# Half of the row maxima from scores and relu of key differences, the gate on GpSimd and ScalarE early, output weights stored one at a time

## The chip, the cores and the metric

The kernel runs on one core of one Trainium2 chip. The metric is the device time of one execution in microseconds (us); the median of three runs is given. Five engines work side by side, each through its own instructions in order: TensorE (PE) multiplies matrices, with its weight loads shown apart as PEld; VectorE (DVE), ScalarE (ACT) and GpSimd (POOL) do the elementwise work; SyncE (SP) issues the DMA transfers here, all on one queue. Results of TensorE land in eight PSUM banks of 128 x 512 numbers; everything else lies in SBUF or in DRAM.

## The reference

Two attention blocks over the same input x (2048 rows, 1024 columns, 32 heads of width 32), mixed by a gate of one number per row:

```python
g = _sigmoid((x * gate_w).sum(-1, keepdims=True))
a = _A_ref(x, A_wqkv, A_wo)      # linear attention
b = _B_ref(x, B_wqkv, B_wo)      # softmax attention
return g * a + (1 - g) * b
```

Block A uses phi(t) = t + 1 for t > 0 and exp(t) otherwise (plus 1e-6), sums kv = phi(k)^T v over all rows, and gives phi(q) kv / (phi(q) . sum phi(k)), then the product with A_wo. Block B is

```python
scores = jnp.einsum("bhqd,bhkd->bhqk", q, k) * (Dh ** -0.5)
p = _softmax(scores, axis=-1)
o = jnp.einsum("bhqk,bhkd->bhqd", p, v)
```

and then the product with B_wo. All of it is float32.

## The kernel before, in words

**Precision and tiles.** A float32 operand is split into a high part (`hi`, a cast on ScalarE) and a low part (`lo`, a subtraction, mostly on VectorE; `split`, L251), and a product is three matmuls: hi x hi, hi x lo, lo x hi (`three`, L143). Most matmuls have 128 x 128 weights and 512 columns; `C` is 512, `P` 128, `NT` = 16 row blocks, `NJ` = 4 slices of 512 rows or keys, `NK` = 8 slices of the inner dimension.

**q/k phase** (L456 to L533). For each of two pairs of 512-row slices, v's first half is computed, and then for eight groups `g` of four heads the seven products of a Strassen scheme over q and k (`PRODUCTS`, L297). The partial sums are put together on VectorE in the quarters s1, u2, u3 of `tmp`, and `qk_out` (L436) splits a finished slice of q or k and stores both parts to `qk_d` through two alternating pairs of `mid` tiles (6 and 7, 8 and 9). During these products a generator `pair_ops` (L401) makes the weights of the next group on POOL, ACT and DVE into a ring of eight slots, and `spill` (L352) stores the split x to `xs`. Each step of a product also advances these generators.

**Streams.** After that, four generators are interleaved by a planner: `linear` (L721), `maxima` (L888), `heads_` (L1018) and `output` (L1233). The planner keeps an estimated clock per engine (`T`, advanced by `use` with a cost), a list of PSUM banks with the time at which each is free (`take`, `give`), and a list of VectorE work that may be put off (`defer`, run by `fill` or forced by `need`). It advances the stream that is furthest behind among those that can start. All of this happens when the program is built: on the chip each engine has one fixed order of instructions.

**linear** runs units, each an output tile of 128 rows by 512 columns: eight slices of three matmuls, 24 in all. The units come in chunks: the second half of v for block B (`v`), the k and v of block A (`kv`), the q of block A (`q`), and block A's output product (`o`). A unit's rows come from `xs` (or `oA_d` for `o`) into one of two tiles `xp_t`, loaded when the unit two before has ended (`load_xp`, L575). The weights of a chunk are loaded during the last two units of the one before (`load_w`, L558) and split (`split_w`, L567). A `v` unit ends with `v_out` (L364): a copy on ScalarE to `mid[10]` or `mid[11]`, and a store. During the units of the first chunk the gate (`gate`, L331) also takes one step each: it loads two halves of 128 rows of x to `tmp` and multiplies them with the gate's weights on VectorE, with the row sum in `tg`.

**mix** (L661). Block A's output weights times kv, head by head, give new weights `wa`. `load_mix` (L649) loads four tiles of A_wo at the third and ninth unit of the first `q` chunk and of the first `o` chunk; `mix`, run between value products of a head, makes four banks, splits them and stores eight tiles of 256 KB to `wa_d`. The `o` chunks wait until all four entries of `mixed` are there and load their weights with `load_wa` (L552).

**maxima** (L888) makes, for each head, the 16 x 4 score tiles of 128 queries by 512 keys, only for their row maxima: a matmul (L902) and a reduction on VectorE (L907) to `mx`, one column per key slice. `rows` (L910) takes the maximum of the four, and writes its negative as two more rows under the head's q. The operands of a head are q's and k's parts stacked in the partition dimension (`load_q`, L853; `load_k`, L864, one slice of 512 keys at a time), so a score tile is one matmul. Two key stacks alternate between heads.

**heads_** (L1018) makes the scores again, transposed (L1053), with the maxima subtracted through those rows, takes the exponential on ScalarE (L1057) to one of seven tiles, adds up the denominators on POOL (L1098, L1102) and VectorE (L1111) and multiplies with v in three groups of 5, 5 and 6 key blocks (L1149), 40, 40 and 48 matmuls. As the key blocks are used up, the slices of the head after next are loaded (L1063). `maxima` runs about one head ahead.

**output** (L1233) multiplies block B's result with B_wo, mixes in block A's with the gate and stores.

## Time and profile before

| | |
|---|---|
| median of three runs | 2904.31 us (2902.01 to 2905.26) |
| profiled execution, total | 2906.63 us |
| its span, first to last instruction | 2904.8 us |
| mean clock granted to TensorE | 0.991 |
| DMA in all | 400.55 MB, 138 GB/s on average |

The page's engine row gives the busy time, the share of the span and the number of instructions. In 40 slices of the span, tenths of busy time and of the granted clock:

```profile
PE   9999989899999999999999999799999999999999
DVE  6667638788888888888888888688888887886522
ACT  5334320566676667666666666456666665666410
PEclk9999999999999999999999999899999999999999
DMA  5957765423332324233323235444455344524542
```

A slice is 72.6 us. The q/k phase takes the first five and a half slices, the first chunk of `linear` the next one and a half, then come `heads_` with `maxima` and `linear`, and from slice 38 on the last output product alone. Busy time of a matmul overlaps with that of the next, since they are pipelined. In a row of the timeline stand the start, the length, the engine, the line, what was written from what, and in brackets the idle time before it with what ended it; "x4" means that several were merged.

### The profile page before, as it was taken

To read this page: it belongs to the slowest core of one execution; us is meant where nothing else is said; L and a number is where in the kernel's file an instruction comes from. 1 tells how busy PE (TensorE), PEld (TensorE's weight loads), DVE (VectorE), ACT (ScalarE), POOL (GpSimd) and SP (SyncE) were. 2 spreads that over 40 slices of the span, in tenths; PEclk is the share of its full clock that TensorE was granted. 3 is DMA by queue.
4 is the path that set the end of the run, shared out by engine and by line. 5 is a ranking of instruction groups with operands and counts; after the bars stand their busy time and mean duration, and the time that the engine had idled before them with its cause. 6 is when DMAs were issued, how large, how long until landed. Compare 5 with 4: busy or idle time off the path is not lost.

```text
span 2904.8 us, 44336 instructions
## 1 busy us (share of the span) xinstructions
PE 2847.1 (98%) x15744; PEld 2039.5 (70%) x15744; DVE 2227.9 (77%) x3715; ACT 1596.8 (55%) x2976; POOL 1853.9 (64%) x646
## 2 busy tenths in 40 slices
PE   9999989899999999999999999799999999999999
PEld 7888867666666766666666666467676666766787
DVE  6667638788888888888888888688888887886522
ACT  5334320566676667666666666456666665666410
POOL 1212220488798889987988888468777878785000
PEclk9999999999999999999999999899999999999999
DMA  5957765423332324233323235444455344524542
GB/s 174 291 173 216 243 202 189 156 91 98 99 117 76 93 88 120 89 102 92 117 80 91 88 120 165 157 166 146 146 175 182 112 146 127 153 88 140 171 158 78
DMA packets 302496, 400.55 MB, mean 138 GB/s; under 512 B 92682, under 2 KB 185354, under 8 KB 299146
## 3 DMA queue, kind: packets, MB, share of 16 engines
q1 hardware_dynamic: 302276, 397.73, 44.3%
q8 instruction: 124, 2.03, 0.3%
q14 instruction: 96, 0.79, 0.1%
HBM read 287.57 MB, written 108.79 MB: 136 GB/s over the span
## 4 chain that ended last, share of the span: by engine, by line
PE 94%; DMA 3%; DVE 2%; ACT 0%; issue 0%; SPq 0%; ACTq 0%; DVEq 0%
PE bank L1053 16%; PE bank L902 16%; PE bank L1149 15%; PE bank L146 11%; PE bank L148 10%; PE bank L147 10%; PE bank L430 3%; PE bank L432 3%; PE bank L431 3%; PE bank L472 1%; PE bank L955 1%; PE bank L470 1%; PE bank L471 1%; DMA big<-xs 1%; DMA big<-qk 0%; PE bank L707 0%
## 5 line engine op out<-in xcount | busy, mean ns | idle before, releaser
L1102 POOL TENSOR_TENSOR big<-big,big 128x1536 f32<-128x1536 f32 (+1 forms) x434 | 1556.5, 3586 | 209.0 <-ACT big L1057 186.9
L907 DVE TENSOR_REDUCE mx<-bank 128x1 f32<-128x512 f32 x2048 | 1308.7, 680 | 306.7 <-PE bank L902 301.8
L1057 ACT ACTIVATE big<-bank 128x512 f32<-128x512 f32 x2048 | 1180.1, 601 | 528.1 <-PE bank L1053 457.8
L902 PE MATMUL bank<-big,big 128*128 128x512 f32 x2048 | 804.8, 393 | 21.6 <-DVE mx L907 11.9
L1053 PE MATMUL bank<-big,big 128*128 128x512 f32 x2048 | 810.7, 397 | 2.2 <-ACT big L1057 2.0
L146 PE MATMUL bank<-big,big 128*128 128x512 f32 x1408 | 554.6, 394 | 25.4 <-DMA big<-xs 21.4
L148 PE MATMUL bank<-big,big 128*128 128x512 f32 x1408 | 552.6, 392 | 1.0 <-DMA big<-oA 0.8
L147 PE MATMUL bank<-big,big 128*128 128x512 f32 x1408 | 552.8, 393 | 0.0
L1053 PEld LDWEIGHTS bank<-big,big 128*128 128x128 f32 x2048 | 384.4, 188 | 159.8 <-issue 62.8
L902 PEld LDWEIGHTS bank<-big,big 128*128 128x128 f32 x2048 | 385.9, 188 | 106.4 <-DVE mx L907 12.6
L1149 PE MATMUL bank<-big,mid 128*32 128x512 f32 x4096 | 459.2, 593 | 0.0
L146 PEld LDWEIGHTS bank<-big,big 128*128 128x128 f32 x1408 | 265.8, 189 | 91.2 <-issue 19.2
L1149 PEld LDWEIGHTS bank<-big,mid 128*32 128x32 f32 x4096 | 127.7, 110 | 263.6 <-issue 263.6
L148 PEld LDWEIGHTS bank<-big,big 128*128 128x128 f32 x1408 | 266.0, 189 | 58.5 <-DMA big<-oA 1.2
L147 PEld LDWEIGHTS bank<-big,big 128*128 128x128 f32 x1408 | 265.9, 189 | 55.4
L1111 DVE TENSOR_TENSOR bank<-bank,big 128x512 f32<-128x512 f32 (+1 forms) x434 | 280.2, 646 | 7.6 <-ACT big L1057 5.7
L1098 POOL TENSOR_TENSOR big<-big,big 128x1536 f32<-128x1536 f32 (+1 forms) x31 | 111.6, 3601 | 264.7 <-issue 141.1
L253 DVE TENSOR_TENSOR big<-mid,big 128x512 fp32r<-128x512 f32 x216 | 152.8, 731 | 83.9 <-ACT big L252 83.8
L409 POOL TENSOR_TENSOR mid<-mid,mid 128x512 f32<-128x512 f32 x16 | 20.7, 1291 | 278.3 <-DVE big L253 265.3
L252 ACT CAST big<-mid 128x512 fp32r<-128x512 f32 x216 | 130.2, 624 | 100.9 <-POOL mid L410 55.3
L431 PE MATMUL bank<-big,big 128*128 128x512 f32 x448 | 174.3, 389 | 0.0
L432 PE MATMUL bank<-big,big 128*128 128x512 f32 x448 | 174.3, 389 | 0.0
(102 smaller groups left out, 1949.8 us busy)
## 6 DMA issues: line engine op xcount, KB each, us to landing
big<-xs SPq DMA_DIRECT2D x208, 512.0 KB
qk<-mid SPq DMA_DIRECT2D x128, 256.0 KB
big<-oA SPq DMA_DIRECT2D x64, 512.0 KB
big<-qk SPq DMA_DIRECT2D x96, 256.0 KB
big<-qk SPq DMA_DIRECT2D x384, 64.0 KB
mid<-in_b_wqkv SPq DMA_DIRECT2D x88, 256.0 KB
xs<-big SPq DMA_DIRECT2D x64, 256.0 KB
oA<-mid SPq DMA_DIRECT2D x64, 256.0 KB
```

What stands on the lines that cost most here:

```text
L146: yield nc.tensor.matmul(ps, sh, mh_, start=(kt == 0), stop=False)
L147: yield nc.tensor.matmul(ps, sh, ml_, start=False, stop=False)
L148: yield nc.tensor.matmul(ps, sl, mh_, start=False, stop=(kt == NK - 1))
L431: nc.tensor.matmul(ps, sh, ml_, start=False, stop=False)
L432: nc.tensor.matmul(ps, sl, mh_, start=False, stop=(i == HK - 1))
L902: nc.tensor.matmul(bank[b], q[:, t * P:(t + 1) * P], k[:, j * C:(j + 1) * C], start=True, stop=True)
L907: nc.vector.tensor_reduce(m[:, t, j:j + 1], bank[b], AX.X, ALU.max)
L1053: nc.tensor.matmul(bank[b], k[:, t * P:(t + 1) * P], q[:, j * C:(j + 1) * C], start=True, stop=True)
L1057: nc.scalar.activation(pr_t[i][:, j * C:(j + 1) * C], bank[b], AF.Exp, scale=SCALE)
L1102: nc.gpsimd.tensor_add(lacc[:, :qp], lacc[:, :qp], pr(t)[:, :qp])
L1111: nc.vector.tensor_add(lacc[:, qp:] if t == NT - 1 else l_b[:, :n], l_b[:, :n], src)
L1149: nc.tensor.matmul(av_b[j * DH:(j + 1) * DH, :], v[:, t, :], pr(t)[:, j * C:(j + 1) * C], start=(t == 0), stop=(t == NT - 1))
```

## The change

- **Maxima.** In the q/k phase the difference of the two key slices of a pair (k of slice 1 minus slice 0, and of 3 minus 2) is also made, split and stored to `kd_d`. In `maxima`, the key stack's slice 1 first holds the difference. For the first 32 score tiles of a head, pairs are made: the score difference goes through a relu on ScalarE to one of two tiles `rise`, and one VectorE instruction adds it to the score of slice 0 and takes the row maximum, since max(s0, s1) = s0 + relu(s1 - s0). The other 32 tiles are reduced as before. `mx` has three columns. When the last of the pairs is issued, slice 1 itself is loaded (`load_k(h, 1, True)`), for the use in `heads_`.
- **Gate.** It runs during the q/k phase, one step per product: load of half a row block, four steps later the product on GpSimd, one step after that the row sum as an accumulated copy on ScalarE. It uses the `rise` tiles, and `tg` lies in `kvb`.
- **Copies of v.** `v_out` in `linear` uses five `mid` tiles in turn.
- **Output weights.** In a `q` chunk the eight stores of `mix` are kept in a list `stores`; one is issued at each key block of a head, what is left at the next `load_mix` or at the first `o` unit. `mixed` counts stores, eight for a set.

```diff
-    tg = sb.tile([P, 2, NT], F32, name="tg")
-    mx = [sb.tile([P, NT, NJ], F32, name=f"mx{i}") for i in range(2)]
+    tg = kvb.rearrange("p k d -> p (k d)")[:, :2 * NT].rearrange("p (i t) -> p i t", t=NT)
+    mx = [sb.tile([P, NT, NJ - 1], F32, name=f"mx{i}") for i in range(2)]
...
+    rise = [sb.tile([P, C], F32, name=f"rise{i}") for i in range(2)]
...
+        steps = [[] for _ in range(3 * 2 * NT + 6)]
+        for n in range(2 * NT):
+            t, i = divmod(n, 2)
+            gx = rise[n % 2]
+            w = zrep[:, i * HD:(i + 1) * HD]
+            steps[3 * n].append(lambda gx=gx, t=t, i=i: nc.sync.dma_start(
+                gx, x[t * P:(t + 1) * P, i * HD:(i + 1) * HD]))
+            steps[3 * n + 4].append(lambda gx=gx, w=w: nc.gpsimd.tensor_mul(gx, gx, w))
+            steps[3 * n + 5].append(lambda gx=gx, t=t, i=i: nc.scalar.activation(
+                gx, gx, AF.Copy, accum_out=tg[:, i, t:t + 1]))
...
                     nc.vector.tensor_add(u3, ps, u3)
-                    qk_out(1, g, js[0], u3)
+                    qk_out(qk_d[1], g, js[0], u3)
+                    nc.vector.tensor_sub(kd, s1, u3)
+                    qk_out(kd_d, g, np_, kd)
...
                 next(side, None)
+                next(gating, None)
...
     def load_mix():
+        while stores:
+            stores.popleft()()
...
                 for p, src in enumerate((hi, lo)):
-                    nc.sync.dma_start(wa_d[p][a][c][:, r * DH:(r + 1) * DH, :], f32(src))
-                mixed.append((a, c))
+                    if lin_kind[0] == "q":
+                        stores.append(lambda p=p, src=src: store(p, src))
+                    else:
+                        store(p, src)
...
-            for _ in range(1 + (n == 1) if n < NT else 0):
-                next(gating, None)
...
-                v_out(c, t, ps, mid[10 + t % 2])
+                v_out(c, t, ps, mid[(10, 11, 7, 8, 9)[n % 5]])
...
+        part = j == 1 and not late
+        src, ss = (kd_d, slice(j // 2 * C, (j // 2 + 1) * C)) if part else (qk_d[1], sl)
...
-            for i in range(NT * NJ):
+            items = []
+            for i in range(NT * NJ // 2):
                 j, t = divmod(i, NT)
...
+                for jj in (2, 3) if j else (1, 0):
...
+                    if j:
+                        fill(end + LATE)
+                        give(b, use("dve", 0.605, end))
+                        nc.vector.tensor_reduce(m[:, t, jj - 1:jj], bank[b], AX.X, ALU.max)
+                    elif jj:
+                        need(items[-2:-1])
+                        end_d = use("act", 0.49, end)
+                        up = rise[i % 2]
+                        nc.scalar.activation(up, bank[b], AF.Relu)
+                        give(b, end_d)
...
+                def largest(_, b=b, up=up, t=t):
+                    nc.vector.tensor_tensor_reduce(up, bank[b], up, 1.0, LOWEST, ALU.add, ALU.max,
+                                                   accum_out=m[:, t, 0:1])
+
+                items.append(defer(largest, max(end, end_d), 0.7, 1))
+                give(b, 0.0, items[-1:])
+                if t == NT - 1:
+                    load_k(h, 1, True)
...
+                    if j == 1 and stores:
+                        stores.popleft()()
```

74 lines of the change are left out of this document (36 added, 38 removed).

## The prediction, made before the changed kernel was run

> **What bounds the kernel now.** I read the page first, then the windows, the waits of the matmul queue, and the timelines around each wait.
>
> ```profile
> span 2904.8 us, 44336 instructions
> ...
> PE 2847.1 (98%) x15744; PEld 2039.5 (70%) x15744; DVE 2227.9 (77%) x3715; ACT 1596.8 (55%) x2976; POOL 1853.9 (64%) x646
> ...
> PE 94%; DMA 3%; DVE 2%; ACT 0%; issue 0%; SPq 0%; ACTq 0%; DVEq 0%
> ```
>
> TensorE (PE) is busy for 2847.1 of 2904.8 us and carries 94% of the chain that ended last. VectorE (DVE) is busy for 77%, and its largest group, the row maxima, is what the change thins out. That saves time only where PE waits for it. Two windows (PE, PEld, DVE, ACT, POOL, clock, DMA share, GB/s), the second inside the attention stage:
>
> ```profile
> 72.60:145.20 72.60, 72.60 (x322) 60.13 (x321) 47.93 (x74) 26.82 (x48) 20.48 (x16) 1.00 0.94 291
> ...
> 1016.70:1089.30 72.60, 72.60 (x468) 48.23 (x470) 60.91 (x105) 45.89 (x88) 63.28 (x22) 1.00 0.29 88
> ```
>
> In both PE has no gap, and 322 matmuls in 72.6 us are one every 0.226 us. So in the attention stage, where nearly all maxima run, a free DVE gives nothing. What can be gained lies in the places where PE stands. The timeline of PE shows the six longest (start, length, what ran, then the idle time before it and its releaser) and two matmuls after one of them:
>
> ```profile
> 424.56 0.79 PE L902 MATMUL bank<-big,big 128*128 128x512 f32 x1 [2.64 <-ACT mid L365]
> 425.15 0.63 PE L147 MATMUL bank<-big,big 128*128 128x512 f32 x1
> 425.58 0.63 PE L148 MATMUL bank<-big,big 128*128 128x512 f32 x1
> ...
> 438.49 0.80 PE L902 MATMUL bank<-big,big 128*128 128x512 f32 x1 [11.86 <-DVE mx L907]
> ...
> 524.97 0.47 PE L146 MATMUL bank<-big,big 128*128 128x512 f32 x1 [2.13 <-DVE big L573]
> ...
> 534.15 0.79 PE L902 MATMUL bank<-big,big 128*128 128x512 f32 x1 [6.85 <-ACT mid L365]
> ...
> 1843.85 0.77 PE L146 MATMUL bank<-big,big 128*128 128x512 f32 x1 [6.37 <-DMA big<-xs]
> ...
> 1887.83 0.77 PE L146 MATMUL bank<-big,big 128*128 128x512 f32 x1 [15.04 <-DMA big<-xs]
> ```
>
> The idle sums to 2.64 + 11.86 + 2.13 + 6.85 + 6.37 + 15.04 = 44.9 us. After it matmuls come 0.43 us apart (425.15, 425.58) instead of 0.226, for 4 + 7, 7, 8 and 8 of them: 34 x 0.2 = 6.8 us more. By place: **A** (near 425 and 438) 14.5 + 2.2 = 16.7 us, **B** (near 525 and 534) 9.0 + 1.4 = 10.4 us, **C** (near 1844 and 1888) 21.4 + 3.2 = 24.6 us; 51.7 us together. The waits of PE hold little else: its next longest in the attention stage is this one.
>
> ```profile
> PE bank L1053 <- ACT big L1057: 2.0, 1, 2.0
> ```
>
> Why PE stands in A and B is in the timelines of SP (the DMA queue), ACT (ScalarE) and DVE:
>
> ```profile
> 420.07 0.38 SPq L366 DMA_DIRECT2D v<-mid  x1
> ...
> 421.91 7.76 SPq L873 DMA_DIRECT2D big<-qk  x12
> ...
> 430.38 2.70 SPq L334 DMA_DIRECT2D big<-in_x  x4
> ...
> 512.69 7.24 SPq L260 DMA_DIRECT2D mid<-in_a_wqkv  x10
> 520.05 0.82 SPq L583 DMA_DIRECT2D big<-xs  x2
> ...
> 522.80 4.54 SPq L260 DMA_DIRECT2D mid<-in_a_wqkv  x6
> ```
>
> ```profile
> 423.92 0.58 ACT L365 COPY mid<-bank 128x512 f32<-128x512 f32 x1 [11.35 <-DMA v<-mid]
> ...
> 529.16 2.06 ACT L571 CAST big<-mid 128x512 fp32r<-128x512 f32 x3 [4.93 <-DMA mid<-in_a_wqkv]
> ```
>
> ```profile
> 434.85 0.69 DVE L344 SCALAR_TENSOR_TENSOR big<-big,zrep 128x512 f32<-128x512 f32 x1 [11.07 <-DMA big<-in_x]
> ```
>
> A: the third copy of v (L365) needs a `mid` tile whose store was issued only at 420.07, behind the first head's loads; then the gate (L344) on DVE waits for x, issued at 430.38 behind the second head's twelve loads, and the maxima queue behind it. B: sixteen weight loads, with the loads of x for the gate among them, make xs (520.05) and the last weights (522.80) late; the copy of v at L365 stands on ACT behind the three casts that ended their wait at 529.16.
>
> C is the burst of eight stores of wa:
>
> ```profile
> 1816.01 0.60 SPq L679 DMA_DIRECT2D wa<-big  x1
> ...
> 1827.02 2.46 SPq L679 DMA_DIRECT2D wa<-mid  x1
> ...
> 1835.75 2.70 SPq L583 DMA_DIRECT2D big<-xs  x2
> ...
> 1868.13 2.40 SPq L679 DMA_DIRECT2D wa<-mid  x1
> ...
> 1881.61 4.59 SPq L583 DMA_DIRECT2D big<-xs  x4
> ```
>
> SP is in them from 1816.0 to 1829.5, some 2.4 us each at the end, then again until 1870.5; the loads of xs stand behind them.
>
> **The change part by part.** Durations are from this run: span 2904.8, execution 2906.63 us, 2.3 above the median of 2904.31.
>
> ```profile
> L907 DVE TENSOR_REDUCE mx<-bank 128x1 f32<-128x512 f32 x2048 | 1308.7, 680 | 306.7 <-PE bank L902 301.8
> L1057 ACT ACTIVATE big<-bank 128x512 f32<-128x512 f32 x2048 | 1180.1, 601 | 528.1 <-PE bank L1053 457.8 <-POOL big L1102 4.1 <-issue 2.6
> ...
> L810 DVE SCALAR_TENSOR_TENSOR bank<-mid,bank 128x512 f32<-128x512 f32 x32 | 22.0, 687 | 1.5 <-ACT bank L590 1.4
> ...
> L344 DVE DVE_READ_ACCUMULATOR big<-big,zrep 128x1 f32 x32 | 2.6, 82 | 0.0
> ...
> L410 POOL TENSOR_TENSOR mid<-mid,mid 128x512 f32<-128x512 f32 x16 | 21.3, 1330 | 1.3
> ```
>
> *Maxima.* The matmuls stay 2048. Per head 32 of the 64 reductions (32 x 0.680 = 21.8 us) go; in come 16 relus on ACT (like L1057, 16 x 0.60 = 9.6 us) and 16 two-input reductions on DVE. These do not occur before: not below 0.680 (L907, the same elements read), not above two such passes, 1.37; I take 0.687 + 0.082 = 0.77 (L810 and the accumulator read), the nearest in operands. DVE loses 21.8 - 12.3 = 9.5 us a head, or 0.1 gained at the upper end. Worth **0** either way, as PE has no gap there. The new wait: the two-input reduction waits for the relu, and behind it on DVE stand other maxima and the sums of the probabilities, then PE for banks.
>
> *Key differences.* Per group of heads and pair one subtraction (0.69), one cast on ACT (0.60), one low part (0.69) and two stores of 256 KB: 16 x 1.38 = 22 us on DVE, 10 on ACT, beside DVE's 47.9 and ACT's 26.8 of 72.6 us in the first window. A fifth user of two pairs of `mid` tiles makes some casts wait for a store; PE's products there go to eight banks in turn, so it feels a lateness above seven products (each 12 matmuls x 0.226 = 2.7 us, so 19 us). Cost **0** while that holds. Late key loads, 3 x 64 KB a head, wait on SP for the last difference matmul, with xs loads behind; that matmul is at PE's front when they are emitted: 0.
>
> *Gate.* 32 products on DVE (22 us) leave A's and B's stretch; 32 loads, 32 products on POOL (like L410, 1.3 us) and 32 sums on ACT (0.6 to 0.7) move into the q/k phase. ACT waits for POOL, POOL for x loaded four products (11 us) earlier; behind ACT's sum stand the casts of q and k, behind POOL's product the next weights. On SP the loads pass the q/k stores, the spill and the weights. Per group (seven products, 19 us) that is two stores of differences, 0.52 MB, and 7/3 loads of x, 0.61 MB: 59 GB/s, onto 291 at a share of 0.94 (310 full): over 87 us of spilling 3.5 MB late, 11 us per pair, 22 in both if nothing hid it. Split weights stand seven products (19 us) ahead, so I take 0 and keep 22 for the range.
>
> *A.* With five tiles instead of two the third and fourth copies of v need no store, and no x load stands in the way. Late next: the first pair of maxima needs two key slices instead of one, loaded behind two more stores. Left: 1 us (0 to 16.7). Gain 15.7.
>
> *B.* Without 512 KB of x per unit (1.8 us at 291 GB/s, twice) the xs load and the last weights come some 3 to 4 us sooner, so the first wait goes and of the second 3 us stay (0 to 10.4). Gain 7.4.
>
> *C.* One store per key block of a head. Between these two groups lies one head of that stage:
>
> ```profile
> 1956.68 5.29 PE bank L1149 x48
> ...
> 2039.29 5.29 PE bank L1149 x48
> ```
>
> That is 82.6 us, 5.2 per block against 2.46 per store, so SP has room between them. But some four stores are left when the second set of output weights is loaded; they go at once (four times 2.4 us), and those loads wait for them. The next xs load follows a unit later. Left: 4 us (0 to 24.6). Gain 20.6.
>
> **Sum**: 15.7 + 7.4 + 20.6 = 43.7. The execution of 2906.6 becomes 2862.9; on the median 2904.3 - 43.7 = 2860.6, rounded to **2860**.
>
> **Rivals.** *Loads stay late* (2872 to 2893, centre 2882). While the stores run, this window reads:
>
> ```profile
> 1825.00:1830.00 5.00, 5.00 (x24) 4.06 (x23) 3.92 (x7) 4.19 (x8) 4.84 (x3) 1.00 0.26 102
> ```
>
> A quarter of the DMA engines' time is used at 102 GB/s, where 0.94 gave 291. If the same quarter serves each store, it is held 2.46 of every 5.2 us, 47%, besides the other traffic, and each xs load ends with its slowest part. If half of C stays (12.3) and 9 of A and B together, the gain is 51.7 - 21 = 31, less 9 of the 22 from the crowded early phase: 22, or 2882. For it: 0.26. Against it: spaced stores let xs wait behind one, not eight.
>
> The Trainium skill (DMA: Bandwidth & Descriptors, "Why a DMA increments its semaphore by 16 and not by 1") says that a transfer is spread over the largest number of engines, up to 16, that divides the slowest dimension of both sides. The store's DRAM side has 4 there, so by it 4 of 16 engines carry it, and spreading in time makes no store shorter; the 0.26 agrees. By that rule the time leans to this rival's, without it to the forecast.
>
> *ACT becomes the bound* (slower). The 48-matmul groups come once a head here too:
>
> ```profile
> 1044.88 5.15 PE bank L1149 x48
> ...
> 1108.06 5.15 PE bank L1149 x48
> ```
>
> A head is 63.2 us. All relus fall into one half of it, 31.6 us, in which ACT now has 45.89/72.6 x 31.6 = 20.0 us, then 29.6. That fits with 2.0 to spare, 0.13 per relu. PE's order is fixed beforehand, so if a relu with its waits takes over 0.73, PE stands; the gain of 43.7 is gone at 43.7/32 = 1.4 us a head, at 0.81 per relu. At 1.0, (16 x 0.27) x 32 = 138 us: 2999; at 0.85, 61 us: 2922. For it: 94% of ACT in that half. Against it: consecutive ACT instructions overlap, two of 0.60 in 1.09 us in its timeline below, and PE has other streams to run.
>
> ```profile
> 534.00 1.09 ACT L1057 ACTIVATE big<-bank 128x512 f32<-128x512 f32 x2
> ```
>
> *The change does not do what it says*: each stall comes back under another releaser, as the same loads run on one queue. Then it is within 6 us of 2904.
>
> **How the numbers follow.** Forecast (2845 to 2872) 0.62; loads stay late 0.21, with 0.19 of it below 2893; stalls return 0.06; ACT bound 0.11. A measurement of this kernel can tell about 0.2%, 6 us. Faster: 0.62 + 0.21 = 0.83; same 0.06; slower 0.11. The range 2845 to 2893 holds 0.81: its low end is all of A, B and C gone (2852.6) with 7 more for small waits and the ones at the end, its high end the bounds of C and of the early phase. As most of the chance is on one side, it stands alone.
>
> **What would show it.** Right: in PE's waits L365, L907 and xs are gone or below 3 us each; the windows from 363 to 581 and from 1815 to 1960 are full at clock 1.00; DVE falls by some 300 us (32 x 9.5; gate and differences cancel), ACT rises by some 340 (32 x 9.6, plus 10 and 21); the 63.2 us between 48-groups stay. Wrong: PE waiting at L902 or L1053 for ACT or the two-input reduction in every head; gaps before 400 us with the DMA share at 1; xs still named as releaser near 1850.

## The result and the profile after

The change made the kernel slower: 2925.36 us (median of four runs, 2924.17 to 2926.06) against 2904.78 (four runs beside them, 2902.01 to 2906.61), a ratio of 1.0071 with a 95% interval of 1.0054 to 1.0089. Forecast were 2860 us, in a range of 2845 to 2893. The profiled execution took 2924.17 us, with a span of 2922.3.

Line numbers are those of the kernel after: the maxima's matmul is L922 (before L902), the transposed scores L1093 (L1053) and their exponential L1097 (L1057), the linear matmuls L149 to L151 (L146 to L148), `split`'s cast and low part L255 and L256, the relu L933, the pair reduction L940, the gate L340 to L343. In the experiments they shift by a few lines.

The page's engine row and chain:

```profile
PE 2870.8 (98%) x15744; PEld 2037.1 (70%) x15744; DVE 1974.5 (68%) x3683; ACT 1807.6 (62%) x3568; POOL 1902.2 (65%) x678
...
PE 81%; ACT 4%; DMA 3%; issue 3%; DVE 2%; POOL 1%; SPq 0%; ACTq 0%; POOLq 0%; DVEq 0%
```

VectorE lost 253 us and ScalarE gained 211, much as meant. PE's part of the chain fell from 94% to 81%, and ScalarE, nothing before, has 4%. The waits of PE (total, times, longest):

```profile
PE bank L149 <- ACT big L255: 8.4, 4, 3.6
PE bank L1093 <- ACT mid L853: 5.8, 1, 5.8
PE bank L473 <- DVE big L512: 4.5, 1, 4.5
...
PE bank L922 <- ACT mid L368: 3.0, 1, 3.0
...
PE bank L149 <- DMA big<-xs: 1.8, 1, 1.8
```

The waits that the change aimed at have shrunk: xs from 21.4 to 1.8 us, the copy of v (L365, now L368) from 9.5 to 3.0, the gate's 11.9 behind L907 is gone. Others stand in their place, most of them on ScalarE. How much each part of the program lost shows better between fixed points of PE's timeline: the first linear matmul, the first transposed score, and the 48-matmul groups at the ends of the first, eighteenth and twenty-first head. Before:

```profile
400.91 0.39 PE L146 MATMUL bank<-big,big 128*128 128x512 f32 x1
...
525.51 0.40 PE L1053 MATMUL bank<-big,big 128*128 128x512 f32 x1
...
593.91 5.34 PE L1149 MATMUL bank<-big,mid 128*32 128x512 f32 x48
...
1688.62 5.34 PE L1149 MATMUL bank<-big,mid 128*32 128x512 f32 x48
...
1956.62 5.36 PE L1149 MATMUL bank<-big,mid 128*32 128x512 f32 x48
```

After:

```profile
423.60 0.39 PE L149 MATMUL bank<-big,big 128*128 128x512 f32 x1
...
542.06 0.39 PE L1093 MATMUL bank<-big,big 128*128 128x512 f32 x1
...
608.11 5.34 PE L1191 MATMUL bank<-big,mid 128*32 128x512 f32 x48
...
1720.32 5.34 PE L1191 MATMUL bank<-big,mid 128*32 128x512 f32 x48
...
1966.22 5.36 PE L1191 MATMUL bank<-big,mid 128*32 128x512 f32 x48
```

The differences of neighbouring starts give this table. Its last two columns are two of the experiments below, from the same five rows of their timelines. Each column is one profiled execution.

| stretch, us | before | after | change | old_maxima | split_stores |
|---|---|---|---|---|---|
| q/k phase, to the first linear matmul | 400.9 | 423.6 | +22.7 | 404.1 | 404.7 |
| to the first transposed score (A, part of B) | 124.6 | 118.5 | -6.1 | 105.0 | 105.5 |
| to the first 48-group (rest of B) | 68.4 | 66.1 | -2.3 | 65.5 | 64.2 |
| 17 heads beside the `kv` chunks | 1094.7 | 1112.2 | +17.5 | 1094.6 | 1094.6 |
| three heads beside the first `q` chunks (C) | 268.0 | 245.9 | -22.1 | 258.9 | 252.9 |
| the rest of the span | 948.2 | 956.1 | +7.9 | 948.7 | 947.7 |
| span | 2904.8 | 2922.3 | +17.5 | 2876.8 | 2869.6 |

C came as forecast. A gave little, and three stretches that the forecast held at zero cost 48 us. The experiments take these apart.

### The profile page after: what moved, and what is told of

Read it like the earlier page. It is cut to its first block, busy times and chain, and to the rows that moved or that the text cites. A ratio compares the mean times of both kernels' runs of the same rounds, so it can differ in the third digit from the quotient of the medians.

```text
span 2922.3 us, 45817 instructions
## 1 busy us (share of the span) xinstructions
PE 2870.8 (98%) x15744; PEld 2037.1 (70%) x15744; DVE 1974.5 (68%) x3683; ACT 1807.6 (62%) x3568; POOL 1902.2 (65%) x678
## 4 chain that ended last, share of the span: by engine, by line
PE 81%; ACT 4%; DMA 3%; issue 3%; DVE 2%; POOL 1%; SPq 0%; ACTq 0%; POOLq 0%; DVEq 0%
PE bank L1093 16%; PE bank L922 15%; PE bank L1191 14%; PE bank L149 11%; PE bank L151 10%; PE bank L150 10%; ACT big L1097 2%; PE bank L995 1%; PE bank L435 1%; ACT rise L933 1%; PE bank L433 1%; PE bank L434 1%; ACT mid L255 1%; DMA mid<-in_b_wqkv 1%; DMA qk<-mid 1%
## 5 line engine op out<-in xcount | busy, mean ns | idle before, releaser
L1097 ACT ACTIVATE big<-bank 128x512 f32<-128x512 f32 x2048 | 1172.2, 615 | 397.1 <-PE bank L1093 363.3
L1093 PE MATMUL bank<-big,big 128*128 128x512 f32 x2048 | 810.0, 398 | 8.5 <-ACT mid L853 5.8
L922 PE MATMUL bank<-big,big 128*128 128x512 f32 x2048 | 806.3, 395 | 8.0 <-ACT mid L368 3.0
L928 DVE TENSOR_REDUCE mx<-bank 128x1 f32<-128x512 f32 x1024 | 654.4, 681 | 157.9 <-PE bank L922 157.2
L940 DVE CUSTOM_DVE_ANT_0 rise<-bank,rise 128x512 f32<-128x512 f32 x512 | 351.2, 688 | 353.4 <-ACT rise L933 208.9
L149 PE MATMUL bank<-big,big 128*128 128x512 f32 x1408 | 555.7, 395 | 14.2 <-ACT big L255 8.4
L150 PE MATMUL bank<-big,big 128*128 128x512 f32 x1408 | 553.0, 393 | 0.8 <-DVE big L256 0.7
L151 PE MATMUL bank<-big,big 128*128 128x512 f32 x1408 | 552.4, 392 | 0.4 <-DVE big L256 0.4
L1093 PEld LDWEIGHTS bank<-big,big 128*128 128x128 f32 x2048 | 385.0, 188 | 169.3 <-issue 61.2
L922 PEld LDWEIGHTS bank<-big,big 128*128 128x128 f32 x2048 | 386.1, 189 | 100.9 <-ACT big L1097 11.9
L933 ACT ACTIVATE rise<-bank 128x512 f32<-128x512 f32 x512 | 317.3, 622 | 30.3 <-PE bank L922 28.4
L149 PEld LDWEIGHTS bank<-big,big 128*128 128x128 f32 x1408 | 265.6, 189 | 80.1 <-ACT big L255 10.5
L151 PEld LDWEIGHTS bank<-big,big 128*128 128x128 f32 x1408 | 265.6, 189 | 58.5 <-issue 0.8
L256 DVE TENSOR_TENSOR big<-mid,big 128x512 fp32r<-128x512 f32 x216 | 166.1, 792 | 83.6 <-ACT big L255 83.3
L255 ACT CAST big<-mid 128x512 fp32r<-128x512 f32 x216 | 130.5, 623 | 93.1 <-POOL mid L413 51.3
L433 PE MATMUL bank<-big,big 128*128 128x512 f32 x448 | 175.8, 392 | 4.2 <-ACT big L255 4.2
```

The source lines that it names most:

```text
L149: yield nc.tensor.matmul(ps, sh, mh_, start=(kt == 0), stop=False)
L150: yield nc.tensor.matmul(ps, sh, ml_, start=False, stop=False)
L151: yield nc.tensor.matmul(ps, sl, mh_, start=False, stop=(kt == NK - 1))
L922: nc.tensor.matmul(bank[b], q[:, t * P:(t + 1) * P], k[:, jj * C:(jj + 1) * C], start=True, stop=True)
L928: nc.vector.tensor_reduce(m[:, t, jj - 1:jj], bank[b], AX.X, ALU.max)
L933: nc.scalar.activation(up, bank[b], AF.Relu)
```

## The experiments

| kernel | what it is | us | ratio to before, 95% interval |
|---|---|---|---|
| old_maxima | after, with the maxima of before | 2881.03 | 0.9907 (0.9892 to 0.9922) |
| kd_out | after, pairs from k of slice 1, no differences made | 2890.81 | 0.9943 (0.9929 to 0.9958) |
| gate_back | after, gate on VectorE as before | 2921.91 | 1.0048 (1.0032 to 1.0065) |
| stores_only | before, single stores | 2899.70 | 0.9971 (0.9960 to 0.9982) |
| maxima_only | before, new maxima and differences | 2952.60 | 1.0153 (1.0138 to 1.0169) |
| relu_narrow | kd_out, relu on 32 of 512 columns | 2877.93 | 0.9896 (0.9881 to 0.9911) |
| casts_dve | kd_out, weight casts of `kv` and `q` on VectorE | 2939.24 | 1.0104 (1.0087 to 1.0121) |
| gate_loads | after, of the gate only the loads | 2909.69 | 1.0005 (0.9995 to 1.0014) |
| gate_pool | after, the gate without its sums | 2919.53 | 1.0043 (1.0028 to 1.0058) |
| no_gate | after without the gate | 2906.19 | 0.9997 (0.9987 to 1.0006) |
| kd_own | no_gate, own tiles for the differences | 2894.73 | 0.9957 (0.9942 to 0.9972) |
| two_stores | old_maxima, two stores per key block | 2882.62 | 0.9908 (0.9894 to 0.9923) |
| split_stores | old_maxima, each store in four | 2869.65 | 0.9871 (0.9857 to 0.9886) |
| before_split | before, each store in four | 2894.63 | 0.9956 (0.9939 to 0.9973) |
| after_split | after, each store in four | 2912.16 | 1.0015 (1.0006 to 1.0025) |
| res_tiles | after, other tiles for block A's result | 2930.27 | 1.0078 (1.0061 to 1.0095) |

### Which part of the change loses

**old_maxima** undoes the maxima and with them the key differences. From after:

```diff
-                    nc.vector.tensor_sub(kd, s1, u3)
-                    qk_out(kd_d, g, np_, kd)
...
-        part = j == 1 and not late
-        src, ss = (kd_d, slice(j // 2 * C, (j // 2 + 1) * C)) if part else (qk_d[1], sl)
+        src, ss = qk_d[1], sl
...
+            for i in range(NT * NJ):
...
+                nc.vector.tensor_reduce(m[:, t, j:j + 1], bank[b], AX.X, ALU.max)
```

> The changed kernel with the maxima as before: four reductions a row block on VectorE, no differences, no relu, no late loads. Gate early, five tiles for v and single stores stay. Theory 3 (the relus fill ScalarE in the kv chunks): a head there falls from 65.4 to 64.4 us, 17 us in all, and with the q/k phase back the time is 2925 - 22 - 17 = about 2886. Rival (the kv chunks slow down for another reason, such as the bank that a pair holds, the moved gate or the stores): they stay at 65.4 and the time is about 2903.

Measured: 2881.03 us. In the table of stretches the 17 heads are back at 1094.6, the q/k phase is 3.2 us longer than before, and the stretch of A is 19.6 us shorter. So the early gate, five tiles and single stores gain 27 us on the 2908.2 of before beside them, and the maxima with their differences lose 44.

**maxima_only** is the counterpart: the kernel before with the maxima and the differences alone. Its diff is the maxima's part of the change.

```diff
+                    nc.vector.tensor_sub(kd, s1, u3)
+                    qk_out(kd_d, g, np_, kd)
...
+                        nc.scalar.activation(up, bank[b], AF.Relu)
...
+                    nc.vector.tensor_tensor_reduce(up, bank[b], up, 1.0, LOWEST, ALU.add, ALU.max,
+                                                   accum_out=m[:, t, 0:1])
```

> The kernel before with the new maxima and the key differences alone: the gate on VectorE beside the first linear chunk, two tiles for v and the burst of eight stores of wa stay as before. If the costs found so far stand by themselves: q/k phase 4 us longer (as in gate_back, first linear matmul near 405), 8 us more up to the first score matmul (gate_back 132.4 against 124.6), 17 us over the heads beside the kv chunks, the idle time near 1850 as before: 2934 to 2944, and no wait for L853's copy near 2250, as the stores go at once. Rival (the maxima lose only together with the single stores or the five tiles): 2908 to 2918.

Measured: 2952.60 us, 45 slower than the 2907.79 beside it, some 9 more than the upper end. The signs were right, but two statements were not: the waits in C came to 25.9 us instead of 21.4, now behind exponentials, and the wait for the result's copy is there without single stores. In its waits of PE the first row is C, the second A, the third the copy:

```profile
PE bank L1082 <- ACT big L1086: 25.9, 2, 13.5
PE bank L911 <- DVE mx L929: 10.2, 2, 9.9
...
PE bank L1082 <- ACT mid L842: 5.8, 1, 5.8
```

**kd_out** makes no differences; the pairs use k of slice 1 itself, so the maxima are of other numbers.

```diff
-                    nc.vector.tensor_sub(kd, s1, u3)
-                    qk_out(kd_d, g, np_, kd)
...
-        src, ss = (kd_d, slice(j // 2 * C, (j // 2 + 1) * C)) if part else (qk_d[1], sl)
+        src, ss = qk_d[1], sl
```

> Leaves out the making, splitting and storing of the key differences; the pairs of maxima, their relu and the late loads stay, with the plain slice 1 in place of the difference, so the maxima are other numbers. Theory 1 (a chain over ScalarE, VectorE and GpSimd paces the q/k phase: one group took 17 to 18 us before and 20.8 us in the changed kernel, where TensorE needs 19.1): the group falls to about 18.3 us, the first matmul of the linear stage starts near 401 us instead of 423.6, and the time falls by 20 to 26 us to about 2902. Theory 2 (the DMA is full in that phase): only 0.52 of 1.14 MB a group go, so about half of the 22.7 us, time near 2914. Both: the 65.4 us a head in the kv chunks stay.

**gate_back** runs the gate on VectorE beside the first linear chunk, as before, with all else of the change.

```diff
-                next(gating, None)
...
+            for _ in range(1 + (n == 1) if n < NT else 0):
+                next(gating, None)
```

> The changed kernel with the gate where it was, on VectorE in the first linear chunk; the rest stays. Theory 1: the group falls only by the gate's share of the chain, about 1 us, to 19.8, so some 10 of the 22.7 us of the q/k phase go; the waits for x near the first maxima come back with about 12 us: time about 2927. Theory 2: more than half of the bytes go, so at least 12 us of 22.7, time about 2924. Kv chunks stay at 65.4 us a head.

Measured: 2890.81 and 2921.91 us. The first linear matmul comes at 403.80 in kd_out and at 405.26 in gate_back, against 400.91 before and 423.60 after. So in the q/k phase the gate alone costs 2.9 us, the differences alone 4.4, and both together 22.7: the costs do not add, there is a slack that holds one of them and not both. Both forecasts missed in part: kd_out gained 35 us where 20 to 26 were expected, and gate_back got 18 us of the phase back where the theory of a chain had some 10. With the pairs still there but no differences, kd_out is 35 us faster than after, yet 10 slower than old_maxima. gate_back gives its gain in the q/k phase back in A, where the first score comes 132.5 us after the first linear matmul.

### What lengthens the q/k phase

**gate_loads** keeps the gate's loads and leaves out its products and sums; **gate_pool** leaves out the sums; **no_gate** leaves out all three. The lines taken out of after:

```diff
-            steps[3 * n].append(lambda gx=gx, t=t, i=i: nc.sync.dma_start(
-                gx, x[t * P:(t + 1) * P, i * HD:(i + 1) * HD]))
-            steps[3 * n + 4].append(lambda gx=gx, w=w: nc.gpsimd.tensor_mul(gx, gx, w))
-            steps[3 * n + 5].append(lambda gx=gx, t=t, i=i: nc.scalar.activation(
-                gx, gx, AF.Copy, accum_out=tg[:, i, t:t + 1]))
```

> The changed kernel, in which of the early gate only the loads of x stay: no product on GpSimd, no sum on ScalarE, the gate is a constant. The bytes of the q/k phase are all there. Theory 1 (chain over the engines): a group falls from 20.8 to about 19.2 us, as with the differences alone; the first linear matmul starts near 405 instead of 423.6 us, and the time is about 2903. Theory 2 (bytes): nothing changes, 2925.

> The kernel after (2925.4 us, first matmul of the linear stage at 423.6 us) with the gate's loads and its products on GpSimd, but without the row sums on ScalarE, so the gate's value is a constant. With loads alone the first linear matmul came at 408.2 and the time was 2909.7. Theory 1 (the row sum on ScalarE is what lengthens a group: it waits for GpSimd's product, and the casts of the next key and query slices stand behind it): first linear matmul at 408 to 412, 2908 to 2914. Rival (the product of 1.45 us on GpSimd does it, ahead of the next group's weights): first linear matmul at 418 to 424, 2919 to 2927. In between, both have a part.

> The kernel after (2925.4 us; first linear matmul at 423.6, first score matmul 118.5 us later) without the gate's loads, products and sums, so the gate's value is a constant; the key differences are made as in after. With the loads alone it was 2909.7, 408.2 and 120.7 us. If the loads cost nothing, as the last two runs suggest: first linear matmul at 404 to 408, the first score matmul still 116 to 121 us later, since the weights of the first linear chunk are cast behind the last key differences, and 2905 to 2911. Rival (the loads take bandwidth from the key stores): the 118 us fall to 106 to 110 and the time to 2890 to 2898.

The first linear matmul comes at 405.92 without the gate, 408.20 with its loads, 419.50 with loads and products and 423.60 with all. Of the gate's 17.7 us, beside the differences, 2.3 are the loads', 11.3 the products' on GpSimd and 4.1 the sums' on ScalarE. The first theory of gate_pool, that the sums do it, falls; so does bandwidth as the cause in gate_loads, though that run ended 7 us above the other theory's 2903. The longest of the waits of GpSimd up to 425 us in after:

```profile
POOL mid L412 <- DVE big L256: 224.4, 16, 48.2
```

Ten of the products stood waiting for their load of x, 37.6 us in all and once for 15.6. But GpSimd is not the engine that is late: before the differences for the next group's weights (L412) it waited 224.4 us in all for low parts on VectorE (L256). What grew with the products is VectorE's own work. Its low parts of the weights up to 425 us, in gate_loads and then in gate_pool (busy, mean ns of one):

```profile
L256 DVE TENSOR_TENSOR big<-mid,big 128x512 fp32r<-128x512 f32 x200 | 142.4, 735 | 70.0 <-ACT big L255 69.9
```

```profile
L256 DVE TENSOR_TENSOR big<-mid,big 128x512 fp32r<-128x512 f32 x197 | 152.3, 796 | 71.0 <-ACT big L255 71.0
```

In the timelines of after such a low part takes 0.67 to 0.69 us where GpSimd is idle, and 1.16 us on average, at most 1.78, where it overlaps a product of the gate. For some 200 of them 61 ns more are 12 us, near the 11.3. That this is how the products cost their time is a reading of the traces; no run tests it by itself.

What a group takes shows on ScalarE, where each group begins with the copy of s1. Its first and its last row of the second eight groups, before and after:

```profile
254.44 0.60 ACT L491 COPY big<-bank 128x512 f32<-128x512 f32 x1
...
384.79 0.59 ACT L491 COPY big<-bank 128x512 f32<-128x512 f32 x1 [0.81 <-PE bank L432]
```

```profile
269.03 0.60 ACT L494 COPY big<-bank 128x512 f32<-128x512 f32 x1
...
419.10 0.57 ACT L494 COPY big<-bank 128x512 f32<-128x512 f32 x1
```

Seven intervals in 130.4 us are 18.6 us each; after, seven in 150.1 are 21.4. PE needs 84 x 0.226 = 19.0 us for a group. Before, the chain over the other engines keeps up with PE; now it is 2.4 us slower. PE doesn't feel that in each group, as weights are split ahead of it: up to 180 us its windows count 773 matmuls in both kernels. It pays where the first eight groups end. Between 180 and 240 us it issues 58 fewer than before, 13 us, and most of the rest is lost after 360 us, where the second eight end. A window at the first of these places, before and after (PE, PEld, DVE, ACT, POOL, clock, DMA share, GB/s):

```profile
210.00:220.00 10.00, 10.00 (x45) 8.28 (x45) 7.56 (x14) 4.82 (x9) 0.00 (x0) 1.00 0.61 173
```

```profile
210.00:220.00 10.00, 5.05 (x20) 3.33 (x19) 7.31 (x12) 3.37 (x7) 2.88 (x2) 0.91 0.78 259
```

There PE waits at L473 for sums on VectorE (L512, L507) and for casts.

### Why A stays

**kd_own** is no_gate with the split of each difference in two tiles of its own.

```diff
-        hi, lo = f32r(mid[6 + n % 2]), f32r(mid[8 + n % 2])
+        if dst is kd_d:
+            hi, lo = f32r(rise[0]), f32r(rise[1])
+        else:
+            n = n_qk[0]
+            n_qk[0] += 1
+            hi, lo = f32r(mid[6 + n % 2]), f32r(mid[8 + n % 2])
```

> no_gate with the split of each key difference in two tiles of its own (the rise tiles, free there without the gate) in place of the two pairs that the four slices of q and k take in turn. Theory 1 (the fifth slice makes the casts on ScalarE wait until a store has read its tile, as in after at 437.0 us with 4.62 us of idle time, and the casts of the next weights stand behind): against no_gate the stretch from the first linear to the first score matmul falls from about 118 to 106 to 109 us, the q/k phase by 1 to 4, the time by 10 to 16. Rival (five splits one behind the other over ScalarE and VectorE set the pace, whatever the tiles): within 4 us of no_gate.

Measured: 2894.73 us, 11.5 below no_gate; the first linear matmul comes 3.0 us earlier (402.95), and the first score 109.8 us behind it instead of 117.2. ScalarE's waits up to 425 us in no_gate, the longest at the last such cast (417.48):

```profile
ACT mid L255 <- DMA qk<-mid: 11.5, 3, 5.4
```

In kd_own that row is gone from the waits. In after the same cast, the last of the phase, starts at 437.00:

```profile
437.00 0.62 ACT L255 CAST mid<-big 128x512 fp32r<-128x512 f32 x1 [4.62 <-DMA qk<-mid]
```

It waits for a store to have read its tile, and the casts of the first chunk's weights stand behind it on ScalarE; PE's longest wait at L149 for L255, 3.65 us at 438.19, follows it. The next, 3.12 us at 432.43, stands behind a cast that waited for the subtraction of the difference on VectorE. So the fifth slice puts waits in front of the linear stage, and its place in the two pairs of tiles is the greater part: 7.4 us in kd_own. A rest of 5 us against old_maxima's 105.0 remains open.

### What the maxima cost in the heads

**relu_narrow** is kd_out with the relu on 32 of 512 columns, so the maxima are not of the scores.

```diff
-                        nc.scalar.activation(up, bank[b], AF.Relu)
+                        nc.scalar.activation(up[:, :DH], bank[b][:, :DH], AF.Relu)
```

> kd_out with each relu on 32 of its 512 columns; order, waits and banks are the same, only ScalarE's time per relu shrinks (about 0.6 to about 0.2 us). The maxima are other numbers. Theory 3 (ScalarE's time in the kv chunks): the 17 us go, a head takes 64.4 instead of 65.4 us there, and the time falls from 2890.8 to about 2874. Rival (the chain relu, then reduction, and the two banks a pair holds): at most 3 us go, time about 2888.

The groups of the three new instructions in after (busy, mean ns of one):

```profile
L940 DVE CUSTOM_DVE_ANT_0 rise<-bank,rise 128x512 f32<-128x512 f32 x512 | 351.2, 688 | 353.4 <-ACT rise L933 208.9 <-PE bank L922 92.8 <-ACT big L1097 14.2
L933 ACT ACTIVATE rise<-bank 128x512 f32<-128x512 f32 x512 | 317.3, 622 | 30.3 <-PE bank L922 28.4 <-DVE mx L940 0.7
...
L940 DVE DVE_READ_ACCUMULATOR2_ANT mx<- 128x1 f32 x512 | 42.3, 83 | 0.0
```

Measured: 2877.93 us, between the two forecasts. In relu_narrow a relu takes 197 ns instead of 622. The windows over the same 17 heads (PE, PEld, DVE, ACT, POOL, clock, DMA share, GB/s) in before, after and relu_narrow:

```profile
593.91:1688.62 1094.71, 1094.71 (x6851) 744.00 (x6849) 937.83 (x1597) 715.99 (x1382) 959.74 (x338) 1.00 0.32 96
```

```profile
608.11:1720.32 1112.21, 1104.89 (x6854) 741.25 (x6850) 796.18 (x1596) 807.75 (x1654) 960.08 (x338) 1.00 0.33 97
...
1138.00:1148.00 10.00, 9.35 (x33) 5.68 (x32) 5.55 (x16) 9.64 (x20) 8.60 (x6) 1.00 0.72 136
```

```profile
573.75:1675.90 1102.15, 1097.56 (x6854) 743.62 (x6851) 796.99 (x1596) 727.75 (x1655) 959.66 (x338) 1.00 0.34 98
```

With cheap relus 10.1 of the 17.5 us are gone; kd_out, with full ones, takes 1112.1 for the stretch like after. So the relus' time on ScalarE is the greater part. It is not lost evenly: averaged over the stretch ScalarE is busy for 73%, but in the window at a change of chunk for 96%, and only 33 matmuls run in 10 us. There ScalarE does relus, exponentials and the casts of the next weights in one line:

```profile
1143.19 0.68 ACT L933 ACTIVATE rise<-bank 128x512 f32<-128x512 f32 x1
1143.66 0.69 ACT L1097 ACTIVATE big<-bank 128x512 f32<-128x512 f32 x1
1144.14 0.72 ACT L577 CAST big<-big 128x512 fp32r<-128x512 f32 x1
```

An instruction starts there every 0.47 to 0.48 us. Head by head, from the starts of the value products in the timelines, the one with this window loses 3.4 us against before (69.2 for 65.8), and the two others of the 17 with such casts 0.8 and 3.0. That makes 7.2 of the 17.5 us; the rest lies in heads without casts of weights, up to 2.1 us in one. Of the whole, 7.4 us stay with short relus; what holds them (the bank of slice 0, kept until its pair is reduced, is one candidate) was not settled.

**casts_dve** tries the obvious remedy on kd_out and moves those casts to VectorE.

```diff
-        nc.scalar.copy(hi, raw)
+        (nc.scalar.copy if eng is nc.vector else nc.vector.tensor_copy)(hi, raw)
```

> kd_out with the casts of new weights at the ends of the kv and q chunks on VectorE instead of ScalarE; the planned order is the same. If ScalarE overflows where these casts fall among the relus (heads that begin near 768, 1095 and 1426 us lose 1 to 5 us more than the others), those 10 us go: time about 2881. If the loss is spread over all relus, or VectorE becomes the one that is late: 2888 or more.

Measured: 2939.24 us, 48 more than kd_out. The groups of the casts in casts_dve, then in kd_out:

```profile
L574 DVE CAST big<-big 128x512 fp32r<-128x512 f32 x27 | 42.8, 1586 | 6.1 <-PE bank L150 5.1 <-issue 0.6 <-POOL big L576 0.3
L574 DVE CAST big<-mid 128x512 fp32r<-128x512 f32 x13 | 21.8, 1676 | 11.2 <-issue 8.3 <-PE bank L150 1.6 <-POOL big L1136 1.3
```

```profile
L574 ACT CAST big<-big 128x512 fp32r<-128x512 f32 x27 | 17.5, 648 | 0.1
```

On average a cast takes 1.59 to 1.68 us on VectorE, beside GpSimd's adds of 3.5 us, and 0.65 on ScalarE. The experiment added a new cost and so doesn't tell what the casts on ScalarE cost.

### The stores of wa

**stores_only** is the kernel before with the `stores` list alone, one store per key block; **two_stores** is old_maxima with two.

```diff
+                    if lin_kind[0] == "q":
+                        stores.append(lambda p=p, src=src: store(p, src))
...
+                    if j == 1 and stores:
+                        stores.popleft()()
```

> The kernel before with the single stores of output weights alone. If the two waits for xs in the first q chunk (21.4 us and 3 us of slow clock) are the burst's, they go as in the changed kernel, which gained 21 us there; and if the wait of 5.8 us for ScalarE's copy in the o chunk (8 us with the slow clock) is theirs as well, it appears here: time about 2892. Rival (a store held by a quarter of the DMA engines keeps xs late anyway): about 2900 or more.

```diff
-                    if j == 1 and stores:
+                    if j in (1, 3) and stores:
```

> old_maxima with two of the eight stores issued at each key block instead of one, so that none is left when the next four weight tiles are loaded. There the multiplication of the second set waited 8.2 us for those loads. If that wait comes from the stores left over, 8 to 10 us go: from 2881 to about 2872. If the stores themselves are what is slow, the wait moves to xs: 2878 or more.

Measured: 2899.70 us, 0.29% under before, and 2882.62, no gain on old_maxima; both forecasts of a larger gain fall. In stores_only PE's waits for xs in this stretch come to 4.1 us instead of 21.4, but the one for A_wo is 8.9; in two_stores A_wo waits 4.3 us and xs 4.9. Issued one by one or faster, the stores move part of the wait. **split_stores** changes the shape of the store instead: four stores of 64 KB with 32 rows each, in place of one whose DRAM side has 4 as its slowest dimension. **before_split** and **after_split** make the same edit in the kernels before and after.

```diff
-                nc.sync.dma_start(wa_d[p][a][c][:, r * DH:(r + 1) * DH, :], f32(src))
+                for i in range(HK):
+                    nc.sync.dma_start(wa_d[p][a][c][i, r * DH:(r + 1) * DH, :], f32(src)[i * DH:(i + 1) * DH, :])
```

> The kernel of old_maxima (maxima as before, gate early, five tiles for v, single stores; 2881.0 us, ratio 0.991) with each 256 KB store of wa issued as four stores of 64 KB, one for each 32 partitions of the tile, so that the slowest dimension has 32 rows instead of 4. Theory 1 (a store is carried by a quarter of the DMA engines: share 0.26 at 102 GB/s while the stores ran before, and the loads of A_wo and xs wait for those engines): the idle time at the two heads in which the second set of output weights is loaded falls from 18 to 6 us or less, and the time to 2867 to 2873. Rival (the wait comes from the order on the queue, where the loads stand behind what is left of the stores, or from the four times as many issues): the idle time stays within 4 us of 18, and the time lies between 2878 and 2886.

> The kernel before (2907 us in these comparisons) with nothing changed but that each store of wa is issued as four of 64 KB; the eight of a set still go at once. Its two waits for xs near 1844 and 1888 came to 21.4 us, stores_only took 7 to 9 us off the time by spreading the stores. Theory 1 (the slow part was a quarter of the engines, not the burst): both waits together fall below 8 us, the time by 14 to 22 us, to 2885 to 2893. Rival (the burst holds the queue for as long, with 32 issues of 0.4 us or more): 2900 to 2908.

> The kernel after (2925.4 us) with each store of wa issued as four of 64 KB, as in split_stores. In after the copy of block A's result waits 6.18 us for a store of wa at 2249.72, and PE issues no matmul from 2245 to 2250, while the DMA engines show a share of 0.26 at 102 GB/s. Theory 1 (the burst of eight stores of the third mix is carried by a quarter of the engines): the wait for the copy falls from 5.8 to 2 us or less, and the time to 2914 to 2920. Rival (the wait is for eight stores in turn on the queue, and 32 issues take as long): the wait stays above 4 us, 2922 to 2928.

Measured: 2869.65, 2894.63 and 2912.16 us, 11, 12 and 13 less than the kernels they start from. PE's waits for A_wo and xs in old_maxima, then for xs in before_split:

```profile
PE bank L677 <- DMA big<-in_a_wo: 8.2, 1, 8.2
...
PE bank L148 <- DMA big<-xs: 2.8, 1, 2.8
```

```profile
PE bank L146 <- DMA big<-xs: 10.4, 2, 9.4
```

The times of split_stores lie in the theory's range, and its waits fall from 11.0 to 3.5 us, 3.1 for A_wo and 0.4 for xs; after_split ends 2 us below its range. before_split ends 2 us above: xs still waits 10.4 us of 21.4, behind eight stores of four issues each on SP. So the shape of a store and the burst each had about half. The Trainium skill (DMA: Bandwidth & Descriptors, "Why a DMA increments its semaphore by 16 and not by 1") gives the rule that the prediction quoted: the number of engines that carry a transfer must divide the slowest dimension of both sides, here 4. The runs agree: 0.26 of the engines' time before, and 3.9 to 11.0 us of waiting less with 32 rows.

**res_tiles** asks whether the new wait at block A's output product (5.8 us at L1093) comes from the tiles of its result, which also hold low parts of the mixed weights.

```diff
-                res = mid[(7, 10)[n % 2]]
+                res = mid[(8, 9)[n % 2]]
```

> The kernel after (2925.4 us) with the results of block A's output product copied to mid[8] and mid[9] instead of mid[7] and mid[10], which hold low parts of the mixed weights until their single stores are through. Theory 1 (this sharing makes the copy at L853 wait, and with it the scores' exponentials on ScalarE and PE: 5.8 us at L1093 near 2250): that wait goes, the idle time of that head falls from 12 to about 3 us, and the time to 2914 to 2919. Rival (the queue itself is late there, with the stores of the third mix and the loads of wa): another releaser takes its place, 2922 to 2928.

Measured: 2930.27 us, so the forecast of this theory falls. The copy itself no longer waits, but tiles 8 and 9 hold the stores of oA, and PE now waits 4.2 us at L149 for oA and 4.2 for an exponential. In after, ScalarE's timeline and a window name the cause:

```profile
2249.72 0.59 ACT L853 COPY mid<-bank 128x512 f32<-128x512 f32 x1 [6.18 <-DMA wa<-mid]
```

```profile
2245.00:2250.00 5.00, 0.00 (x0) 0.00 (x0) 0.41 (x1) 0.28 (x1) 0.00 (x0) 0.92 0.26 102
```

The copy waits for a store of wa, the exponentials stand behind it on ScalarE, and PE starts no matmul in 5 us, while the DMA engines show the same 0.26 at 102 GB/s as in C. In after_split the copy's wait fell from 5.8 to 1.9 us:

```profile
PE bank L1094 <- ACT mid L854: 1.9, 1, 1.9
```

So the slow store is this wait's cause. The copy waits for such a store in maxima_only too (5.8 us of PE), and not in before or old_maxima, so that it stands just there goes with the order that the planner makes for the new maxima.

## Why the prediction was wrong

| step | forecast, us | in after | alone or with the cause taken away |
|---|---|---|---|
| Key differences and gate in the q/k phase | 0, 22 kept for the range | +22.7 | 4.4 and 2.9 |
| A | -15.7 | -6.1, with a little of B | -19.6 in old_maxima |
| B | -7.4 | -2.3 | -2.9 in old_maxima |
| Maxima | 0 | +17.5 | +7.4 with short relus |
| C | -20.6 | -22.1 | -9.1 in old_maxima, -15.1 in split_stores |
| not named | 0 | +7.9 | wait of 5.8 falls to 1.9 in after_split |

**Key differences and gate** is the first step that failed. The text said that a lateness is felt only above seven products, and that split weights stand seven products ahead; it took 0. That is right of one late instruction and wrong of a chain that loses 2.4 us in every group: over the eight groups of one pair of slices that is 19 us, the whole lead, and PE pays at the end of each eight. The two edits were weighed one by one against the same slack, and each would have passed (2.9 and 4.4 us); together they cost 22.7. The 22 us kept for the range had nearly the right size by luck: they rested on DMA bytes, and the gate's loads cost 2.3. GpSimd's products, beside which VectorE's low parts run longer, cost 11.3, and ScalarE's sums 4.1.

**A** was right as to its cause: with the stores and the gate's loads out of the way the stretch falls by 19.6 us. "Late next" was wrong. The text looked at key slices and took 1 us; late were the casts of the first chunk's weights, behind a fifth split that waits for a tile and for its subtraction. The prediction had named that wait ("makes some casts wait for a store") and then priced it at nothing, without asking what stands behind the last of them.

**B** kept 3.0 us at the copy of v, as the text had it; its other part cannot be told apart in these stretches.

**Maxima**: worth 0, "as PE has no gap there". That shows that nothing can be gained, not that nothing can be lost. The prices were right (0.688 + 0.083 against 0.77 for the pair reduction; 0.62 for a relu), and the rival that ScalarE becomes the bound had the mechanism. It had a chance of 0.11, and its sum, 29.6 of 31.6 us in one half of a head, left the casts of the weights out. The three heads with these casts lost 7.2 us of the 17.5; what fills or holds the others, with 10.3, stays open, short relus taking away 10.1 of the whole.

**C** came within 2 us of the forecast. The rival "loads stay late" was right about the store: a quarter of the engines carries it. It cost its part in old_maxima, where the second set's A_wo loads were issued at 1822.87, right behind the stores, and PE waited 8.2 us for them. In after they came at 1876.21, 36 us behind the last store (1840.08), by an order that the prediction didn't foresee; that C came so close is in part luck. The store cost again in the wait at block A's output product, which no step named.

The forecast of VectorE (-300 us) and ScalarE (+340) was met by -253 and +211; the relus' group alone is 317.3 us, so they overlap other instructions in the count of busy time.

split_stores, the change without the new maxima and with split stores, is the best version: 2869.65 us, 1.3% below before, with the forecast's 2860 ten away.

## What to carry to other kernels

A bounding engine without gaps says that freeing another engine gains nothing there, while every instruction added to an engine that feeds it can still lose: add up each feeding engine over the fullest stretch, changes of weights included. Slack is used up jointly, so price all edits of a stage together, as what they add to one period of its slowest in-order chain, longer instructions on the engines beside them included, and ask of every new wait what stands last behind it. Before spreading slow transfers in time, look at their shape: the DMA share and the GB/s while nothing else runs tell how many engines carry one.

## What the runs showed of the hardware

- A cast of 128 x 512 from SBUF to SBUF took 1.59 to 1.68 us on average on VectorE while GpSimd added large tiles, 0.65 us on ScalarE. The Trainium skill (SBUF — State Buffer, "Who interferes with whom") says that a cast on VectorE can use a port pair that it shares with GpSimd, and that whoever is second waits until the other's instruction has ended. The trace of casts_dve agrees: a cast took 0.41 us where GpSimd was idle (the first row), and 2.77 us where an add of GpSimd's ran from 811.10 to 814.58; it ended 0.28 us behind that.

```profile
809.36 0.41 DVE L574 CAST big<-big 128x512 fp32r<-128x512 f32 x1
...
812.09 2.77 DVE L574 CAST big<-big 128x512 fp32r<-128x512 f32 x1
```

- An accumulated copy on ScalarE is two instructions, a copy and a read of the accumulator, which adds 187 ns to 630, as the groups of after show:

```profile
L343 ACT ACTIVATE rise<-rise 128x512 f32<-128x512 f32 x32 | 20.2, 630 | 15.5 <-POOL rise L342 15.5
L343 ACT ACTIVATION_READ_ACCUMULATOR rise<-rise 128x1 f32 x32 | 6.0, 187 | 0.0
```

- The pair reduction on VectorE, one operand in PSUM and one in SBUF, took 688 ns, hardly more than the one-operand reduction of 681 in the same run.
